# The first token tile arrives turned by a DMA transpose, the second tile's load changes queue, two weight loads become one, and a strip's first blocks are pulled forward

## The chip, the cores and the metric

The kernel runs on one core of one Trainium2 chip. The metric is the device time of one execution in microseconds (us). The kernel before takes 215.7 us (median of 6 executions, 215.33 to 216.21). Times inside an execution are counted from the span's start. One execution differs from the next by some tenths of a microsecond, so a profile (one execution) is used to find where time goes, and six executions in turn with the kernel before are used to say how much.

## The reference, cut to what matters

```python
def reference(...):                      # x: 1 x 2048 x 640, bf16
    g = sigmoid((x * gate_w).sum(-1, keepdims=True))
    a = A(x, ...)                        # complex state space: Bu = x @ B_bar, scan over time, y = h @ C + x * Dskip
    b = gelu(x @ w1 + b1) @ w2 + b2      # w1: 640 x 1728, w2: 1728 x 640
    return g * a + (1 - g) * b
```

The opening of the kernel computes the first 768 columns of `x @ w1` for the first 512 tokens. TensorE contracts over the partition axis, so it needs x turned (features on partitions), while x lies in memory with tokens on partitions. D = 640 features are five *strips* of 128. The 512 tokens are four *token tiles* of 128. A *turn* is a matmul with the identity that turns one 128x128 piece of x; VectorE or ScalarE then copies it out of PSUM.

## The kernel before: the parts that matter

The loads of the opening. `nc.sync` is SyncE's DMA queue, `nc.scalar` ScalarE's. `w1a[kd]` holds strip kd of the first 768 columns of w1 (192 KB), `w1b` the next 512, `w1c` the last 448 and one gate column.

```python
    w1b = [const.tile([P, cut2 - cut1], BF16, name=f"w1b_{kd}") for kd in range(KD)]
    w1c = [const.tile([P, n1c], BF16, name=f"w1c_{kd}") for kd in range(KD)]
    # ... cut ...
    load_x0(nc.sync, 0, 1, 0, KA * P)         # token tile 0, first 256 features (64 KB)
    load_w1a(nc.scalar, 0)                    # first strip's weights
    load_x0(nc.sync, 1, 2, 0, KA * P)         # token tile 1
    load_w1a(nc.scalar, 1)                    # second strip's weights
    load_x0(nc.sync, 2, 3, 0, KA * P)
    load_x0(nc.scalar, 0, H, KA * P, D)
    # ... cut: tile 3, w1a[2], three rows of parameters, the rest of x, w1a[3:5], parameters for the biases ...
    for kd in range(KD):
        nc.sync.dma_start(out=w1b[kd][:], in_=B_w1[kd * P:(kd + 1) * P, cut1:cut2])
    for kd in range(KD):
        nc.sync.dma_start(out=w1c[kd][:, 0:F - cut2], in_=B_w1[kd * P:(kd + 1) * P, cut2:F])
```

The order of TensorE's work. `turn_first(a, ..)` turns the first two strips of token tile a; `part(kd, a)` is six matmuls of 128 columns: strip kd of token tile a, for six blocks of output features.

```python
    pA = bank()
    for n in (512, 512, 512, 512, 512, 128, 128, 128, 128):          # warm-up, on constants
        nc.tensor.matmul(pA[:, 0:n], lhsT=ones(P), rhs=ones(n), start=True, stop=True)
    # ... cut ...
    turn_first(0, pA)
    # ... cut ...
    for _ in range(3):                                               # three more on constants
        nc.tensor.matmul(banks[0][:, 0:P], lhsT=ones(P), rhs=ones(P), ...)
    part(0, 0)
    turn_first(1, pA)
    part(1, 0)                                                       # the first user of w1a[1]
    turn_first(2, pA)
    part(0, 1)
    part(1, 1)
    turn_first(3, pA)
    part(0, 2)
    part(1, 2)
    nc.tensor.matmul(pA[:, 0:3 * KS], lhsT=prmA[:], rhs=ident[:, 0:3 * KS], ...)     # "prmA turn"
    # ... cut: the other turns and parts; these go on to part(2, 2) ...
    part(2, 3)
    # ... cut ...
    for kf in range(FA):                                             # FA = 6
        if kf == 3:
            nc.tensor.matmul(pA[:, 0:NB], lhsT=prmB[:], ...)         # "prmB turn"
            nc.vector.tensor_copy(out=colB[:], in_=pA[:, 0:NB])
            for j in range(KD):                                      # gate-column copies, out of PSUM bank pA
                nc.vector.tensor_copy(out=w1c[j][:, n1c - 1:n1c], in_=pA[:, j:j + 1])
        for kd in (4, 3):
            ff1_mm(banks[kf], 0, kf, kd, 0, CH, False, 3)
    # ... cut ...
    two_banks = [bank(), bank()]                                     # the second one is pA's bank again
    for kd in range(KD):
        for i in range(2):
            ff1_mm(two_banks[i], 0, FA + i, kd)                      # the first users of w1b
```

Of the kernel before, what the change touches and what calls it, by code (L numbers as in the profile page):

```python
# [12 lines left out]
BF16 = mybir.dt.bfloat16  # L13
# [3 lines left out]
P = 128  # L17
T = 2048
D = 640
F = 1728  # L20
CH = 512
NCH = T // CH
KD = D // P
# [6 lines left out]
HT = H * P  # L30
# [11 lines left out]
def kernel(  # L42
# [19 lines left out]
    nc = tc.nc  # L62
    x2d = A_x.flatten_outer_dims()
# [3 lines left out]
    const = ctx.enter_context(tc.tile_pool(name="const", bufs=1))  # L67
# [7 lines left out]
    def bank(dtype=F32):  # L75
        return ps.tile([P, CH * 4 // (4 if dtype == F32 else 2)], dtype, name="bank")
# [4 lines left out]
    cut2 = FB * P  # L81
    n1c = F - cut2 + 1
    xT = [const.tile([P, KD, CH], BF16, name=f"xT{c}") for c in range(NCH)]
# [1 line left out]
    w1a34 = const.tile([P, 2, cut1], BF16, name="w1a34")  # L85
    w1a += [w1a34[:, j, :] for j in range(2)]
    w1b = [const.tile([P, cut2 - cut1], BF16, name=f"w1b_{kd}") for kd in range(KD)]
    w1c = [const.tile([P, n1c], BF16, name=f"w1c_{kd}") for kd in range(KD)]
    w2_sb = const.tile([P, KF - 1, D], BF16, name="w2_sb")
    BT_re, BT_im = ([const.tile([P, KD, n * P], BF16, name=f"BT_{ri}{n}") for n in (KSA, KS - KSA)] for ri in ("re", "im"))  # L90
    CT_re = const.tile([P, KS, D], BF16, name="CT_re")
# [34 lines left out]
    def load_w1a(queue, kd):  # L126
        queue.dma_start(out=w1a[kd][:], in_=B_w1[kd * P:(kd + 1) * P, 0:cut1])
# [4 lines left out]
    KA = 2  # L132
    xn[0] = xnp.tile([P, TPC, D], BF16, name="xn")

    def load_x0(queue, a0, a1, d0, d1):
        queue.dma_start(out=xn[0][:, a0:a1, d0:d1], in_=x2d[a0 * P:a1 * P, d0:d1].rearrange("(a p) d -> p a d", p=P))

    load_x0(nc.sync, 0, 1, 0, KA * P)
    load_w1a(nc.scalar, 0)
    load_x0(nc.sync, 1, 2, 0, KA * P)  # L140
    load_w1a(nc.scalar, 1)
    load_x0(nc.sync, 2, 3, 0, KA * P)
    load_x0(nc.scalar, 0, H, KA * P, D)
# [12 lines left out]
    rows(nc.sync, prmB[0:KS, :], gate_w)  # L156
    for kd in range(KD):
        nc.sync.dma_start(out=w1b[kd][:], in_=B_w1[kd * P:(kd + 1) * P, cut1:cut2])
    for kd in range(KD):
        nc.sync.dma_start(out=w1c[kd][:, 0:F - cut2], in_=B_w1[kd * P:(kd + 1) * P, cut2:F])  # L160
    make_identity(nc, ident[:])
    HC = CH // 8
# [16 lines left out]
        nc.sync.dma_start(out=w2_sb[:, k0:k1, :], in_=B_w2[k0 * P:k1 * P, :].rearrange("(kf p) d -> p kf d", p=P))  # L179
    for h in range(2):  # L180
        nc.sync.dma_start(out=w2l[h * F_LAST:(h + 1) * F_LAST, :], in_=B_w2[(KF - 1) * P:F, :])
    nc.sync.dma_start(out=b2bc[:], in_=B_b2.rearrange("(o d) -> o d", o=1).to_broadcast([P, D]))
    nc.sync.dma_start(out=Dbc[:], in_=A_Dskip.rearrange("(o d) -> o d", o=1).to_broadcast([P, D]))
    nc.sync.dma_start_transpose(out=xT[2][:], in_=x2d[2 * CH:3 * CH, :])
# [32 lines left out]
    def pe(cols):  # L217
        ck.pe += cols / 2400.0 + 0.002
# [9 lines left out]
    pA = bank()  # L228
# [3 lines left out]
    def turn(p, col, a, kd):  # L232
        nc.tensor.matmul(p[:, col:col + P], lhsT=xn[0][:, a, kd * P:(kd + 1) * P], rhs=ident[:], start=True, stop=True,  # L233
                         skip_group_check=True)

    def turned(engine, p, col, a, k0, k1):
        dst = xT[0][:, k0:k1, a * P:(a + 1) * P]
        src = p[:, col:col + (k1 - k0) * P].rearrange("p (k t) -> p k t", t=P)
        if engine is nc.vector:
            nc.vector.tensor_copy(out=dst, in_=src)  # L240
        else:
            nc.scalar.activation(out=dst, in_=src, func=ACT.Identity)  # L242

    def turn_first(a, other):
        t = bank()
        turn(t, 0, a, 0)
        turned(nc.vector, t, 0, a, 0, 1)
        turn(other, a * P, a, 1)
        turned(nc.scalar, other, a * P, a, 1, 2)

    turn_first(0, pA)

    def col(name, dtype=F32, n=KS):
        return const.tile([P, n], dtype, name=name)
# [9 lines left out]
    def ff1_mm(p, c, kf, kd, t0=0, t1=CH, first=None, last=KD - 1):  # L264
        w, f0 = (w1a, 0) if kf < FA else (w1b, FA) if kf < FB else (w1c, FB)
        w = w[kd][:, (kf - f0) * P:(kf - f0 + 1) * P]
        nc.tensor.matmul(p[:, t0:t1], lhsT=w, rhs=xT[c][:, kd, t0:t1],  # L267
                         start=(kd == 0) if first is None else first, stop=(kd == last), skip_group_check=first is not None)
        pe(t1 - t0)
# [53 lines left out]
    banks = [bank() for _ in range(FA)]  # L323

    def strip(kd, t0, t1, first, f0=0, f1=FA):
        for kf in range(f0, f1):
            ff1_mm(banks[kf], 0, kf, kd, t0, t1, first, 3)
# [26 lines left out]
    def part(kd, a):  # L354
        strip(kd, a * P, (a + 1) * P, kd == 0)
# [28 lines left out]
    nc.vector.tensor_tensor(out=red, in0=u, in1=kk[:], op=ALU.subtract)  # L384
    part(2, 1)
    part(2, 2)
    part(2, 3)
    nc.scalar.activation(out=FSC[:, 0:KS, 0:NP], in_=red, func=ACT.Sin, scale=TWO_PI_M)
    nc.vector.scalar_tensor_tensor(out=ab, in0=red, scalar=-1.0, in1=red, op0=ALU.mult, op1=ALU.max)
    nc.scalar.activation(out=FSC[:, KS:2 * KS, 0:NP], in_=ab, func=ACT.Sin, scale=-TWO_PI_M, bias=halfpi[:])  # L390
    for kf in range(FA):
        if kf == 3:
            nc.tensor.matmul(pA[:, 0:NB], lhsT=prmB[:], rhs=ident[:, 0:NB], start=True, stop=True, skip_group_check=True)  # L393
            nc.vector.tensor_copy(out=colB[:], in_=pA[:, 0:NB])
            for j in range(KD):
                nc.vector.tensor_copy(out=w1c[j][:, n1c - 1:n1c], in_=pA[:, j:j + 1])
        for kd in (4, 3):
            ff1_mm(banks[kf], 0, kf, kd, 0, CH, False, 3)
    for kf in range(FA):
        ff1_act(banks[kf], 0, kf)  # L400
    two_banks = [bank(), bank()]
# [336 lines left out]
```

## Time and profile before

| | before |
|---|---|
| median of 6 executions | 215.7 us (215.33 to 216.21) |
| profiled execution, its span | 215.48 us, 213.7 us |
| TensorE busy | 210.0 us, 98% of the span |
| VectorE busy | 189.0 us, 88% |
| second strip's weights: issued, landed | 1.15 us, 4.28 us |
| first real block; first block of the second strip | 4.01 us; 4.69 us |

The busy table of the kernel before (engine, busy us, share of the span, instructions):

```profile
span 213.7 us, 3596 instructions
PE 210.0 (98%) x1407; PEld 126.1 (59%) x1407; DVE 189.0 (88%) x387; ACT 103.2 (48%) x186; POOL 1.0 (0%) x13
```

The chain of waits of the kernel before (start us, us, what) shows the opening's one hole, before the last blocks of the third strip:

```profile
8.68 0.39 ACT xT L242
...
9.10 0.30 DVE xT L240
...
9.45 1.79 PE bank L267 x12
```

ScalarE's copy, then VectorE's copy of token tile 3 must end first. And VectorE's timeline at the gate-column copies:

```profile
11.40 0.41 DVE L396 CAST w1c<-bank 128x1 bf16<-128x1 f32 x5
```

All five copies run at once; none waits for a load.

### The profile page before, as it was taken

What the parts mean: (1) busy time and instruction counts of PE and PEld (TensorE: products, weight loads), DVE (VectorE), ACT (ScalarE), POOL (GpSimd) and SP (SyncE); (2) the same over time, 40 slices, a digit from 0 to 9 for tenths busy, and PEclk for the clock granted to TensorE, in tenths of its full rate; (3) what the DMA queues carried; (4) which work ended last, traced back from release to release, by engine and by line L of the source; (5) the groups of instructions that cost most, each with busy time, mean ns of one, the idle gap of its engine ahead of it and who ended that gap; (6) DMA issues with size and microseconds to landing.
All of it is one profiled execution on the core that took longest, in us unless ns stands there. A gap on an engine that the chain in (4) does not pass through costs nothing.

```text
span 213.7 us, 3596 instructions
## 1 busy us (share of the span) xinstructions
PE 210.0 (98%) x1407; PEld 126.1 (59%) x1407; DVE 189.0 (88%) x387; ACT 103.2 (48%) x186; POOL 1.0 (0%) x13
## 2 busy tenths in 40 slices
PE   8999999999999999999999999999999999999994
PEld 5845444454576644775457777444457687676773
DVE  2689999999998999999999999999999999993153
ACT  3699856675758588203563210455682422305100
POOL 1000000000000000000000000000000000000000
DMA  6859999998000000051000005100000000100011
GB/s 196 236 133 182 228 172 267 337 204 219 1 0 0 3 0 0 17 178 67 0 0 3 0 0 187 61 0 2 3 0 14 0 3 31 61 34 0 0 66 61
DMA packets 31571, 15.84 MB, mean 74 GB/s; under 512 B 22978, under 2 KB 31554, under 8 KB 31554
## 3 DMA queue, kind: packets, MB, share of 16 engines
q1 hardware_dynamic: 30850, 14.99, 28.8%
q10 hardware_dynamic: 704, 0.62, 0.9%
q8 instruction: 11, 0.18, 0.4%
q14 instruction: 6, 0.05, 0.1%
HBM read 7.48 MB, written 2.62 MB: 47 GB/s over the span
## 4 chain that ended last, share of the span: by engine, by line
PE 98%; DVE 0%; ACT 0%; issue 0%
PE bank L605 27%; PE bank L267 26%; PE bank L664 20%; PE bank L546 20%; PE bank L230 1%; PE bank L621 1%; PE bank L293 1%; PE bank L233 1%; ACT xT L242 0%; DVE ot L669 0%; PE bank L358 0%; DVE xT L240 0%; PE bank L283 0%; PE bank L393 0%; PE bank L368 0%
## 5 line engine op out<-in xcount | busy, mean ns | idle before, releaser
L605 PE MATMUL bank<-w_sb,gel 128*128 128x384 bf16 (+1 forms) x416 | 57.9, 299 | 0.0
L605 PEld LDWEIGHTS <-gel 128*128 128x128 bf16 x416 | 40.3, 98 | 17.0 <-issue 0.8
L549 ACT ACTIVATE bu<-bank 128x512 bf16<-128x512 f32 x40 | 23.6, 597 | 37.6 <-PE bank L546 37.6
L272 ACT ACTIVATE gel<-bank,colB 128x512 bf16<-128x512 f32 x52 | 33.9, 692 | 11.1 <-PE bank L267 10.8
L664 PEld LDWEIGHTS <-hs 128*128 128x128 bf16 x330 | 31.7, 98 | 11.6
L500 DVE TENSOR_TENSOR_SCAN g<-r_c,carry,v 128x512 bf16<-128x512 f32 x30 | 37.2, 1269 | 0.0
L613 ACT ACTIVATE gb<-bank,gcol 128x384 f32<-128x384 f32 (+1 forms) x32 | 15.1, 525 | 33.6 <-PE bank L605 16.8
L267 PE MATMUL bank<-xT,w1a 128*128 128x512 bf16 (+1 forms) x174 | 28.1, 315 | 0.1
L664 PE MATMUL bank<-CT_im,hs 128*128 128x320 bf16 (+2 forms) x165 | 27.1, 295 | 0.0
L664 PE MATMUL bank<-CT_re,hs 128*128 128x320 bf16 (+2 forms) x165 | 27.1, 295 | 0.0
L669 DVE SCALAR_TENSOR_TENSOR ot<-bank,gcol,gb 128x320 bf16<-128x320 f32 (+2 forms) x33 | 17.4, 533 | 9.9 <-PE bank L664 9.5
L546 PE MATMUL bank<-xT,BT_re 128*128 128x512 bf16 x100 | 24.8, 379 | 0.0
L546 PE MATMUL bank<-xT,BT_im 128*128 128x512 bf16 x100 | 24.8, 379 | 0.0
L267 PEld LDWEIGHTS <-w1a 128*128 128x128 bf16 x174 | 14.5, 99 | 11.8 <-issue 0.2
L267 PE MATMUL bank<-xT,w1b 128*128 128x512 bf16 x80 | 17.9, 379 | 0.0
L546 PEld LDWEIGHTS <-BT_im 128*128 128x128 bf16 x100 | 9.8, 98 | 11.8
L579 DVE TENSOR_TENSOR bank<-xn,Dbc 128x320 f32<-128x320 bf16 (+2 forms) x33 | 14.5, 481 | 2.3 <-ACT gb L613 2.3
L546 PEld LDWEIGHTS <-BT_re 128*128 128x128 bf16 x100 | 9.6, 98 | 11.0
L481 DVE TENSOR_TENSOR v<-wa,wb 128x512 bf16<-128x512 bf16 x40 | 15.2, 421 | 0.6
L594 ACT ACTIVATE bank<-b2bc 128x384 f32<-128x384 bf16 (+1 forms) x24 | 11.7, 524 | 7.3 <-DVE ot L669 7.3
L481 DVE TENSOR_TENSOR wa<-TCOS,g 128x1024 bf16<-128x1024 bf16 x20 | 13.7, 685 | 0.1
L267 PE MATMUL bank<-xT,w1c 128*128 128x512 bf16 x60 | 13.7, 379 | 0.0
(99 smaller groups left out, 166.1 us busy)
## 6 DMA issues: line engine op xcount, KB each, us to landing
out_dram<-ot SPq DMA_DIRECT2D x15, 160.0 KB, 1.8
w_sb<-in_B_w_dram SPq DMA_DIRECT2D x1, 2080.0 KB
xn<-in_A_x_dram SPq DMA_DIRECT2D x3, 640.0 KB
w1b<-in_B_w_dram SPq DMA_DIRECT2D x5, 128.0 KB, 4.2
w1c<-in_B_w_dram SPq DMA_DIRECT2D x5, 112.0 KB, 4.9
w1a<-in_B_w_dram ACTq DMA_DIRECT2D x2, 192.0 KB, 3.1
w1a<-in_B_w_dram SPq DMA_DIRECT2D x1, 384.0 KB, 3.4
xn<-in_A_x_dram SPq DMA_DIRECT2D x4, 64.0 KB, 3.2
```

The source lines that it names most:

```text
L267: nc.tensor.matmul(p[:, t0:t1], lhsT=w, rhs=xT[c][:, kd, t0:t1], start=(kd == 0) if first is None else first, stop=(kd == last), skip_grou ...
L272: nc.scalar.activation(out=gel[c][:, kf, :], in_=p[:, :], func=ACT.Gelu_apprx_tanh, bias=b1_c[:, kf:kf + 1])
L481: nc.vector.tensor_tensor(out=o, in0=a, in1=b, op=op)
L500: nc.vector.tensor_tensor_scan(s["g"][:, ri, :], r_c[:, ks:ks + 1].to_broadcast([P, CH]), s["v"][:, ri, :], init, ALU.mult, ALU.add)
L546: nc.tensor.matmul(p[:], lhsT=BT[ks >= KSA][:, kd, (ks % KSA if ks < KSA else ks - KSA) * P:][:, 0:P], rhs=xT[c][:, kd, :], start=(kd == 0 ...
L549: nc.scalar.activation(out=bu[:, ri, :], in_=p[:], func=ACT.Identity)
L579: dve_now(ck.pe, 0.45, lambda: nc.vector.tensor_tensor(out=p[:, 0:d1 - d0], in0=xn[c][:, a, d0:d1], in1=Dbc[:, d0:d1], op=ALU.mult))
L594: nc.scalar.activation(out=v, in_=src, func=ACT.Identity)
L605: nc.tensor.matmul(p[:, col:col + d1 - d0], lhsT=gel[c][:, kf, a * P:(a + 1) * P], rhs=w2_sb[:, kf, d0:d1], start=False, stop=False, skip_ ...
L613: nc.scalar.activation(out=gbs[ti][:, d0:d1], in_=p[:, col:col + d1 - d0], func=ACT.Identity, scale=gcol[:, 1, ti:ti + 1])
L664: nc.tensor.matmul(p[:, 0:d1 - d0], lhsT=hs[c][:, j, lo:lo + P], rhs=CT[:, j % KS, d0:d1], start=False, stop=(j == 2 * KS - 1), skip_group ...
L669: nc.vector.scalar_tensor_tensor(out=ot[:, d0:d1], in0=p[:, 0:d1 - d0], scalar=gcol[:, 0, ti:ti + 1], in1=gbs[ti][:, d0:d1], op0=ALU.mult, ...
```

## The change

The intent: the first two turns and their copies leave the opening (the DMA brings token tile 0 already turned), the second token tile comes by ScalarE's queue, between the two weight loads, and three half blocks of the fifth strip fill the hole at 9.2 us. The plain copy of tile 0's 256 features, which the output stages need, is loaded later; two w1c loads become one, so the number of loads stays the same.

```diff
-    w1c = [const.tile([P, n1c], BF16, name=f"w1c_{kd}") for kd in range(KD)]
+    w1c = [const.tile([P, n1c], BF16, name=f"w1c_{kd}") for kd in range(3)]
+    w1c34 = const.tile([P, 2, n1c], BF16, name="w1c34")
+    w1c += [w1c34[:, j, :] for j in range(2)]
@@ the opening's loads
-    load_x0(nc.sync, 0, 1, 0, KA * P)
+    nc.sync.dma_start_transpose(out=xT[0][:, 0:KA, 0:P], in_=x2d[0:P, 0:KA * P])
     load_w1a(nc.scalar, 0)
-    load_x0(nc.sync, 1, 2, 0, KA * P)
+    load_x0(nc.scalar, 1, 2, 0, KA * P)
     load_w1a(nc.scalar, 1)
@@ after the w1b loads
-    for kd in range(KD):
+    nc.sync.dma_start(out=w1c34[:, :, 0:F - cut2], in_=B_w1[3 * P:KD * P, cut2:F].rearrange("(k p) f -> p k f", p=P))
+    for kd in range(3):
         nc.sync.dma_start(out=w1c[kd][:, 0:F - cut2], in_=B_w1[kd * P:(kd + 1) * P, cut2:F])
@@ later loads
+    load_x0(nc.sync, 0, 1, 0, KA * P)
@@ TensorE
-    turn_first(0, pA)
@@ before the last part of the third strip
+    AHEAD = 3
+    strip(KD - 1, 0, HT, False, 0, AHEAD)
     part(2, 3)
@@
-            ff1_mm(banks[kf], 0, kf, kd, 0, CH, False, 3)
+            ff1_mm(banks[kf], 0, kf, kd, HT if kd == 4 and kf < AHEAD else 0, CH, False, 3)
```

## The prediction

> **What bounds it now.** TensorE: busy 210.0 of 213.7 us (busy table); the chain of waits is 98% PE. Beyond the opening its only hole over 0.2 us is at 9.17-9.45 us (timeline): the last third-strip blocks wait for VectorE's copy of token tile 3, itself behind a ScalarE copy. Opening: warm-ups end at 3.3 us, when tile 0's rows land; two PE turns and two copies follow, and the first real block starts at 4.01 us. VectorE is nearly as full: from 11.3 to 191 us it idles once, 0.96 us (timeline, waits).
>
> **What the change does.**
> - Opening: two turns and two copies of tile 0 go; a 128x256 DMA transpose comes. The trace has that size (gelL): 1.17 us on SyncE's queue, 3.1 us to landing; free of traffic its last increment came 2.3 us after issue. Issued at 0.73 beside the first weight load (landed 3.5), I estimate a landing at 3.5-3.9. First block 4.01 -> about 3.8: gain 0.1-0.25 us. TensorE's own saving is two 128-column turns, 0.11 us. (The Trainium skill, "VectorE: DVE Perf Modes", the three transpose paths, gives 1309 ns by DMA against 390 ns on TensorE; here queue and landing make it longer, so it pays only because loading was waited for anyway.)
> - The hole: three 256-column blocks of strip five (3 x 109 ns, half of a 512-column block's 216 ns spacing) fill about 0.28 us, if their weights, which landed at 8.4, are there. SyncE's queue moves back 0.2-0.6 us (longer issue; each issue reuses the semaphore of the eighth before it, and the order changed), so they land at about 8.9, just in time. prmA's third row may cost 0-0.3 us the same way.
> - Opening gain on TensorE, net: about 0.3 us (0 to 0.5).
>
> **The hidden cost.** The fourth and fifth blocks of w1c become one tile, loaded by one DMA. VectorE writes the gate column into that tile; in the built program this copy now waits for that DMA's full count, where before it waited for none (11.4 us). In before the first w1c loads landed at 13.9 and 14.2: 15 of 16 increments came by 11.9-12.2, the last about 2 us later, because an instruction fetch of 16 KB held one DMA engine from 10.4 to 12.3 (packet list). The Trainium skill, "DMA: Bandwidth & Descriptors", on why a DMA increments by 16, says only the full 16 means all has landed; this trace agrees. So VectorE should stop at about 11.4 for 1 to 3 us, likely 2.3. Having no idle time to give back, it stays late until 191 us.
>
> **What lateness costs.** TensorE needs VectorE's seeds at the start of each output stage. Slack (timeline): seed done 84.2, needed 86.4; 121.0/123.0; 172.8/174.1. Smallest: 1.3 us. So time changes by about max(-gain, lateness - 1.3): with 2.3 us of lateness +1.0; with 1 us or less -0.3. The tables' copies on ScalarE move about 1 us; banks absorb that.
>
> **Prediction.** 216.5 us (before 215.99), range 215.3 to 217.6; faster by over 2%: 0.01; within 2%: 0.96; slower by over 2%: 0.03.
>
> **What would show it.** First block at 3.7-3.9; no hole before 9.5; VectorE idle at the gate-column copy, released by the w1c DMA, 1-3 us; output stages (around 86, 123, 174) preceded by TensorE waits for seeds, summing to 0-1.5 us, most at the third.
>
> **What would make it wrong.** The w1c DMA landing by 12.3, because the fetch falls elsewhere: then 215.6. The transpose landing after 4.1, the prmA row or fifth-strip weights late: opening gain gone. A late fourth-or-fifth w1b load (landed 13.6, needed 14.1) stalling TensorE. Hidden slack in VectorE that I read as full.

## More of the kernel before

TensorE is the bound, so a microsecond in which it stands, or works slower than it could, is a microsecond of the result. Its timeline in the opening (start us, us, engine and line, output from inputs, shape, count):

```profile
4.01 0.73 PE L267 MATMUL bank<-xT,w1a 128*128 128x128 bf16 x6
4.58 0.28 PE L233 MATMUL bank<-ident,xn 128*128 128x128 bf16 x2
4.69 0.50 PE L267 MATMUL bank<-xT,w1a 128*128 128x128 bf16 x6
...
5.29 0.83 PE L267 MATMUL bank<-xT,w1a 128*128 128x128 bf16 x12
5.96 0.28 PE L233 MATMUL bank<-ident,xn 128*128 128x128 bf16 x2
...
6.74 0.17 PE L368 MATMUL bank<-ident,prmA 128*128 128x15 bf16 x1
```

Matmuls overlap, so read rates from starts, not from the busy column. The twelve blocks of 5.29 take until 5.96: 0.67 us, or 56 ns each. The first six take 0.57 us, 95 ns each on average; read one by one in the trace, they start 107 ns apart until 4.58 us. So TensorE runs at half rate to 4.58 us and at full rate after it. The Trainium skill, "TensorE: Matmul & The Clock Gate", Part 1, section "What's actually happening", describes this: TensorE starts at half clock, and a free-running window of about 3.4 us of activity decides when it gets the full one. The spacings here (107 ns, then 56 ns, for 128 columns) agree.

## The result, and the profile after

The changed kernel takes 217.84 us (217.21 to 218.08, 6 executions) against 215.7 us; ratio 1.0095, 95% interval 1.0073 to 1.0117. A ratio in this document is the mean time of one kernel's runs over the mean of the other's in the same rounds, so it is not quite the ratio of the medians quoted. The change costs 2.1 us, and the time lies outside the predicted range of 215.3 to 217.6.

The busy table after:

```profile
span 215.8 us, 3582 instructions
PE 211.0 (98%) x1397; PEld 128.1 (59%) x1408; DVE 188.7 (87%) x386; ACT 102.7 (48%) x185; POOL 1.0 (0%) x13
PEclk9999999999999999999999999999999999999999
```

TensorE is busy 1 us longer. The row of the granted clock says full speed in every slice: it does not show the half rate that we are about to see. The trace's clock records begin only where the full clock begins (9.16 us here), and time without a record is counted as full. TensorE's timeline after:

```profile
3.92 0.80 PE L269 MATMUL bank<-xT,w1a 128*128 128x128 bf16 x6
4.51 0.42 PE L237 MATMUL bank<-ident,xn 128*128 128x128 bf16 x2
5.47 0.82 PE L269 MATMUL bank<-xT,w1a 128*128 128x128 bf16 x6 [0.54 <-DMA w1a<-in_B_w_dram]
...
6.30 1.49 PE L269 MATMUL bank<-xT,w1a 128*128 128x128 bf16 x12
7.58 0.42 PE L237 MATMUL bank<-ident,xn 128*128 128x128 bf16 x2
7.79 1.49 PE L269 MATMUL bank<-xT,w1a 128*128 128x128 bf16 x12
9.07 0.22 PE L370 MATMUL bank<-ident,prmA 128*128 128x15 bf16 x1
9.15 0.33 PE L237 MATMUL bank<-ident,xn 128*128 128x128 bf16 x3
9.31 0.50 PE L269 MATMUL bank<-xT,w1a 128*128 128x128 bf16 x6
```

Two things are new. TensorE stands before the second strip: its last matmul before starts at 4.62, the next at 5.47, and the profile names the second strip's weights. And the twelve blocks of 6.30 take until 7.58: 1.28 us, 107 ns each, where before they took 56 ns. Half rate now lasts until 9.15 us. The chain of waits after says how the weights came late (the chain reads about 0.15 us later than the timeline for TensorE, because it goes by ends):

```profile
0.73 0.38 ACTq L129
...
1.14 0.46 ACTq L138
...
1.62 3.81 DMA w1a<-in_B_w_dram
...
5.47 0.82 PE bank L269 x6
...
11.03 1.44 PE bank L269 x22
```

On ScalarE's queue the second strip's weights now come third, behind the first strip's weights (L129) and token tile 1 (L138). They are issued at 1.62 instead of 1.15 and land at 5.43 instead of 4.28. The last line shown answers to the hole of before: 22 blocks in one piece, no copy in the chain. The filling works.

SyncE's queue before, and then after:

```profile
0.73 1.84 SPq L136 DMA_DIRECT2D xn<-in_A_x_dram  x4
6.38 2.26 SPq L158 DMA_DIRECT2D w1b<-in_B_w_dram  x5
```

```profile
0.73 1.29 SPq L140 DMA_TRANSPOSE xT<-in_A_x_dram  x1
7.76 2.26 SPq L160 DMA_DIRECT2D w1b<-in_B_w_dram  x5
```

The transpose holds the queue for 1.29 us (a plain load for about 0.4), and by the w1b loads this queue is 1.4 us late. The transpose is not the only reason: in two kernels below that have token tile 1 on ScalarE's queue and no transpose, these loads start at 7.01 (e2) and 7.50 (e11). VectorE's timeline after, at the gate-column copies:

```profile
13.50 0.28 DVE L400 CAST w1c<-bank 128x1 bf16<-128x1 f32 x3
14.11 0.23 DVE L400 CAST w1c<-bank 128x1 bf16<-128x1 f32 x2 [0.33 <-DMA w1c<-in_B_w_dram]
```

This is the wait that the prediction announced, for the merged tile's load, but it is 0.33 us and not 1 to 3, because VectorE itself comes 2 us later.

Cut at TensorE's landmarks (starts in the two profiles), the 2.1 us lie here:

| stretch | before | after | difference |
|---|---|---|---|
| to the first block of the second strip | 4.69 | 5.47 | +0.78 |
| from there to the prmA turn | 2.05 | 3.60 | +1.55 |
| prmA turn to prmB turn | 4.33 | 4.10 | -0.23 |
| prmB turn to the first `BT` matmul (the stage after the opening) | 9.60 | 9.60 | 0 |
| from there to the last matmul | 190.06 | 190.06 | 0 |
| sum | 210.73 | 212.83 | +2.10 |

Everything after 13 us is only shifted. A standstill costs 0.78, the half rate 1.55, and the filled hole gives 0.23 back. (From start to start the standstill is 0.85 us; taking off the 0.11 us that the matmul before it needs at half rate leaves 0.74 idle.)

### The profile page after: what moved, and what is told of

It reads as the page before. It is cut to its first block, busy times and chain, and to the rows that moved or that the text cites. A ratio compares the mean times of both kernels' runs of the same rounds, so it can differ in the third digit from the quotient of the medians.

```text
span 215.8 us, 3582 instructions
## 1 busy us (share of the span) xinstructions
PE 211.0 (98%) x1397; PEld 128.1 (59%) x1408; DVE 188.7 (87%) x386; ACT 102.7 (48%) x185; POOL 1.0 (0%) x13
## 4 chain that ended last, share of the span: by engine, by line
PE 96%; DMA 2%; ACTq 0%; issue 0%; DVE 0%
PE bank L269 27%; PE bank L609 26%; PE bank L668 20%; PE bank L550 20%; DMA w1a<-in_B_w_dram 2%; PE bank L625 1%; PE bank L295 1%; PE bank L237 1%; ACTq L138 0%; ACTq L129 0%; DVE ot L673 0%; PE bank L285 0%; PE bank L370 0%; PE bank L397 0%
## 5 line engine op out<-in xcount | busy, mean ns | idle before, releaser
L269 PE MATMUL bank<-xT,w1a 128*128 128x512 bf16 (+2 forms) x173 | 29.6, 328 | 0.9 <-DMA w1a<-in_B_w_dram 0.5
L269 PEld LDWEIGHTS <-w1a 128*128 128x128 bf16 x177 | 16.2, 108 | 12.4 <-DMA w1a<-in_B_w_dram 0.8
```

Of the source, the lines that this page charges most:

```text
L269: nc.tensor.matmul(p[:, t0:t1], lhsT=w, rhs=xT[c][:, kd, t0:t1], start=(kd == 0) if first is None else first, stop=(kd == last), skip_grou ...
```

## The experiments

Three theories for the standstill and what follows it. *Order*: the weights are late because token tile 1 stands ahead of them in ScalarE's queue. *Transpose*: they are late because the transpose's traffic slows everything. *Clock*: the standstill itself is small, and costs more because it makes the full rate come later. After the first four runs a fourth was needed: *merged tile*, a second penalty that the first one hides.

One table has the landmarks of all profiled executions. "Weights" is when the last part of the second strip's weights landed; "full rate" is the first start from which 128-column matmuls come 56 ns apart (where that falls into a standstill, the first start after it); the three columns after are landmarks of TensorE as above. BT to the last matmul was 190.05 or 190.06 us in every kernel, but 190.22 in e8.

| kernel | weights | full rate | prmA turn | prmA to prmB | prmB to BT | profiled us |
|---|---|---|---|---|---|---|
| before | 4.28 | 4.58 | 6.74 | 4.33 | 9.60 | 215.48 |
| after | 5.43 | 9.15 | 9.07 | 4.10 | 9.60 | 217.61 |
| e1_weights_first | 4.22 | 4.61 | 7.34 | 4.32 | 10.72 | 217.21 |
| e2_no_transpose | 5.95 | 6.0 | 7.90 | 4.06 | 10.25 | 217.08 |
| e3_transpose_alone | 4.14 | 9.53 | 9.46 | 4.37 | 9.60 | 218.32 |
| e4_filler | 5.77 | 4.0 | 7.72 | 4.19 | 10.77 | 217.53 |
| e5_strip_alone | 4.21 | 5.63 | 7.08 | 4.06 | 9.60 | 215.52 |
| e6_w1c_merged | 4.34 | 6.31 | 7.43 | 4.33 | 9.81 | 216.47 |
| e8_merged_gate_from_sbuf | 4.55 | 5.35 | 7.03 | 4.34 | 9.59 | 215.99 |
| e9_after_unmerged | 5.75 | 10.05 | 9.39 | 4.31 | 9.60 | 218.20 |
| e7_weights_first_unmerged | 4.09 | 4.33 | 7.31 | 4.06 | 9.60 | 215.88 |
| e10_filler_unmerged | 5.86 | 3.98 | 7.82 | 4.07 | 9.60 | 216.38 |
| e11_order_alone | 6.40 | 6.45 | 8.36 | 4.33 | 9.60 | 217.08 |
| e12_strip_three_fillers | 4.25 | 5.23 | 7.10 | 4.05 | 9.60 | 215.56 |
| e13_standstill_alone | 4.12 | 3.60 | 8.03 | 4.33 | 9.60 | 216.75 |
| e14_standstill_filled | 4.11 | 3.98 | 7.80 | 4.33 | 9.59 | 216.50 |
| e15_early_pair_filled | 4.17 | 6.10 | 7.85 | 4.05 | 9.60 | 216.39 |

All fifteen kernels are correct, all were timed in five rounds, and "before" was 215.65, 215.79, 215.71 and 215.57 us in the four sets of runs (e1 to e4; e5, e6, e8, e9; e7, e10, e11, e12; e13 to e15). The sets ran on three different chips, so times of different sets are compared only where the difference is far larger than these 0.2 us.

### e1_weights_first: the changed kernel with the old order on ScalarE's queue

```diff
-    load_x0(nc.scalar, 1, 2, 0, KA * P)
     load_w1a(nc.scalar, 1)
+    load_x0(nc.scalar, 1, 2, 0, KA * P)
```

> The changed kernel, but ScalarE's queue issues both weight loads before the second token tile, as in before; the DMA transpose stays. In the changed kernel the second weight load (w1a, second strip) landed at 5.43 us instead of 4.31, TensorE stood still for it and then ran at half speed until 9.1 us. Theory QUEUE ORDER (the 64 KB put ahead of it and its later issue delay it): lands by 4.4 us, second strip starts by 4.8 us, time 215.2 to 216.0. Theory TRANSPOSE (the transpose on SyncE's queue holds up what ScalarE's queue issues after it): still lands after 4.9 us, time 217 or more. Theory of my prediction (VectorE late through the merged w1c tile): if TensorE starts on time, VectorE waits 1 to 3 us at the gate-column copies and the time is 216 to 217.

Measured: 217.89 us (217.2 to 218.28), ratio 1.0102 (1.0086 to 1.0119). The weights land at 4.22, the full rate is there within the first six blocks (from 4.61), and the prmA turn is 1.7 us earlier than in the changed kernel. And the time is the same. The gain was given back at 13 us, which is where TensorE waits in this kernel (engine, line, what it waited for: us in total, times, longest):

```profile
PE bank L269 <- DVE w1c L400: 0.9, 1, 0.9
PE bank L269 <- DMA xT<-in_A_x_dram: 0.7, 1, 0.7
```

The second line is the transpose, landing at 4.43 here. The first is new: a w1b block waits for a gate-column copy of VectorE. So the order is what made the weights late, and something else keeps the time where it was.

### e2_no_transpose: the changed kernel with token tile 0 loaded and turned as before

```diff
-    nc.sync.dma_start_transpose(out=xT[0][:, 0:KA, 0:P], in_=x2d[0:P, 0:KA * P])
+    load_x0(nc.sync, 0, 1, 0, KA * P)
...
+    turn_first(0, pA)
```

> The changed kernel without the transpose: tile 0's rows come by SyncE's queue and are turned on TensorE as in before; the second tile stays on ScalarE's queue ahead of the second weight load. QUEUE ORDER: the second weight load lands after 5.0 us, time 217 or more. TRANSPOSE: it lands by 4.7 us (64 KB more ahead of it, about 0.25 us at the 300 GB/s of that stage), time 215.3 to 216.2. Merged-tile theory: with TensorE on time, VectorE waits 1 to 3 us at the gate-column copies, time up to 217.

Measured: 217.37 us (216.66 to 218.28), ratio 1.0083 (1.0062 to 1.0104). The weights still land at 5.95 and TensorE still stands before the second strip (0.9 us put down to the weights). The theory that the transpose's traffic makes the weights late falls. In this execution the full rate came during the standstill, and again TensorE waited for a gate-column copy, 0.5 us.

### e3_transpose_alone: the kernel before with the transpose and nothing else

```diff
-    load_x0(nc.sync, 0, 1, 0, KA * P)
+    nc.sync.dma_start_transpose(out=xT[0][:, 0:KA, 0:P], in_=x2d[0:P, 0:KA * P])
...
+    load_x0(nc.sync, 0, 1, 0, KA * P)      # after the w2 loads
...
-    turn_first(0, pA)
```

> Before, with the transpose alone: tile 0's first 256 features turned by DMA, its rows loaded later, all else as in before (second tile on SyncE's queue behind the transpose). TRANSPOSE: the second weight load lands after 4.9 us, or the second tile's rows do, and the time is 217 or more. QUEUE ORDER: weights land by 4.5 us; the second tile's rows, issued at about 2.0 us instead of 1.2, land at about 5.0 instead of 4.06, so TensorE still waits up to 0.5 us; time 215.8 to 216.8.

Measured: 216.31 us, ratio 1.0059 (1.0026 to 1.0091), in two groups: four executions at 216.22 to 216.33, two at 218.02 and 218.32. The profile is one of the late ones. The weights land at 4.14, the transpose at 4.33, and TensorE waits for it (0.6 us) and then for token tile 1 behind it in SyncE's queue (0.5 us). In that execution the full rate came at 9.53 us. So the transpose alone does not pay: it lands about 1 us after a plain load of the same piece (3.29 in the kernel before).

### e4_filler: the changed kernel with eight blocks on constants where TensorE stands

```diff
     turn_first(1, pA)
+    for _ in range(8):
+        nc.tensor.matmul(banks[0][:, 3 * P:4 * P], lhsT=ones(P), rhs=ones(P), start=True, stop=True, skip_group_check=True)
     part(1, 0)
```

> The changed kernel with eight idle 128-column matmuls (ones by ones, into columns that are overwritten later) between the second tile's turns and the second strip, so that TensorE does not stand still while the second weight load is awaited. CLOCK theory (the standstill of 0.85 us keeps TensorE at half speed 4.5 us longer, about 1.5 us of the loss; the wait itself is 0.8): spacing of 128-column matmuls falls from 107 to 56 ns by 6 us, time about 216.3. If the half speed has nothing to do with the standstill: spacing stays 107 ns until 9 us, time 217.8 as the changed kernel.

Measured: 217.59 us (217.39 to 217.7, 4 executions), ratio 1.0089 (1.0076 to 1.0103). TensorE's timeline:

```profile
4.00 0.49 PE L269 MATMUL bank<-xT,w1a 128*128 128x128 bf16 x6 [0.20 <-DMA xT<-in_A_x_dram]
...
4.45 0.63 PE L364 MATMUL bank<-const-bfloat16-1.0 128*128 128x128 bf16 x8
5.82 0.51 PE L269 MATMUL bank<-xT,w1a 128*128 128x128 bf16 x6 [0.74 <-DMA w1a<-in_B_w_dram]
...
13.23 0.38 PE L269 MATMUL bank<-xT,w1b 128*128 128x512 bf16 x1
14.61 1.25 PE L269 MATMUL bank<-xT,w1b 128*128 128x512 bf16 x5 [1.00 <-DVE w1c L402]
```

In this execution TensorE has its full rate already at 4.00, before the fillers begin, so the profile cannot show that the fillers brought it. What it does show is the worth of an early full rate: the prmA turn is 1.35 us earlier than in the changed kernel (7.72 against 9.07) although the weights land 0.34 us later. And it shows where that goes. Between the first and the second w1b block 1.38 us pass (blocks of this size come about 216 ns apart elsewhere). VectorE's timeline has the reason:

```profile
12.24 0.28 DVE L402 CAST w1c<-bank 128x1 bf16<-128x1 f32 x3
14.33 0.23 DVE L402 CAST w1c<-bank 128x1 bf16<-128x1 f32 x2 [1.81 <-DMA w1c<-in_B_w_dram]
```

The fourth copy writes into the merged tile and waits for its load, which lands at 14.30. The copies read PSUM bank pA, and the second w1b bank is that same bank. TensorE may not start there before the fifth copy has read it. This is the second penalty: it holds the stage after at 22.2 to 22.7 us, whether or not the opening is late. In the changed kernel, where TensorE gets there 1.3 us later, it is hidden.

### e5_strip_alone: the kernel before with the fifth strip's early blocks

```diff
     part(2, 2)
+    AHEAD = 3
+    strip(KD - 1, 0, HT, False, 0, AHEAD)
     part(2, 3)
...
-            ff1_mm(banks[kf], 0, kf, kd, 0, CH, False, 3)
+            ff1_mm(banks[kf], 0, kf, kd, HT if kd == 4 and kf < AHEAD else 0, CH, False, 3)
```

> Before with one part alone: three half blocks of the fifth strip put before the last third-strip blocks, to fill the standstill at 9.17 to 9.45 us. The weights of the fifth strip landed at 8.4 us in before, so they are there. Prediction's term: 0.25 us faster, about 215.4 where before is 215.65; the gap before the last third-strip blocks shrinks from 0.35 us spacing to under 0.25 of anything but work. Rival (the hole is a latency that moves along behind the inserted work): no change.

Measured: 215.58 us (215.46 to 215.76), ratio 0.9994 (0.9982 to 1.0006). The stretch from prmA to prmB shrinks by 0.27 us, as predicted for this part. In the time nothing can be told from zero; in the profiled execution the full rate came 1 us later than in the kernel before's, and the prmA turn 0.34 us later with it, which is more than the hole gives back.

### e6_w1c_merged: the kernel before with the two w1c loads merged

The edit is the first and third hunk of the change.

> Before with one part alone: the fourth and fifth w1c blocks in one tile loaded by one DMA, issued before the other three. BANK theory (formed from the experiments with the weights first and with the filler, where TensorE stood 0.9 to 1.5 us before its second w1b matmul, released by the gate-column copy): that copy waits for the DMA, and the bank that it reads is the one TensorE needs next; so TensorE, which would need it at about 12.5 us, waits until the DMA has landed, at 13.9 to 14.3 us: 1.2 to 1.7 us slower, about 217.1. Theory of my prediction (no direct wait; only VectorE's lateness at the output stages, less 1.3 us of slack): 216.0 to 216.9, TensorE without a gap at 12 to 14 us and with gaps at about 86, 123 and 174 us.

Measured: 216.52 us (216.29 to 217.16), ratio 1.0042 (1.0026 to 1.0059). VectorE waits 0.8 us for the merged load (landed 13.20), and the weight load of a w1b block waits 0.5 us for the copy; prmB to BT grows by 0.22 us. Of the 0.99 us between the two profiled executions that is a quarter. The rest, 0.69 us, is lost before the prmA turn, with full rate at 6.31. It would probably not have been won with an earlier full rate: the wait ends with the landing at 13.20, so a TensorE that came 0.69 us earlier would have waited that much longer at the same bank (an estimate from this profile, not a run).

### e8_merged_gate_from_sbuf: the same, with the copies reading SBUF

```diff
-                nc.vector.tensor_copy(out=w1c[j][:, n1c - 1:n1c], in_=pA[:, j:j + 1])
+                nc.vector.tensor_copy(out=w1c[j][:, n1c - 1:n1c], in_=colB[:, j:j + 1])
```

> The merged w1c tile on before, but the gate columns are copied from the SBUF copy of the column values and no longer from the PSUM bank, so TensorE gets that bank as soon as the column copy is done, while VectorE still waits for the merged load. BANK theory alone: no gap on TensorE at 12 to 14 us, time near before (215.5 to 215.9) as far as the later slack holds. My prediction's slack reading: VectorE stops 1.5 to 2.5 us and stays late, the first output stages wait for seeds, time = before + (lateness - 1.3 us), so 215.9 to 216.9, with TensorE gaps at about 86, 123 or 174 us.

Measured: 216.44 us (215.99 to 216.55), ratio 1.0031 (1.0017 to 1.0045). VectorE still waits 0.9 us for the load, but TensorE does not wait for VectorE any more, and prmB to BT is back at 9.59. This shows the path of the cost: the PSUM bank. It also tests the prediction's path, VectorE's lateness reaching the output stages: no wait for VectorE's seeds appears there with 0.9 us of lateness. That is under the slack of 1.3 us that the prediction read, so it neither breaks nor makes the rule. (The 0.16 us more between BT and the last matmul go to one pause before 84 us that the profile puts down to instruction issue.) In time the kernel gains next to nothing over e6_w1c_merged, so what its executions lose stays unexplained. The profiled one is the fastest of the six; the five others took 216.09 to 216.55 and left no trace, so a later loss through VectorE is not ruled out there.

### e9_after_unmerged: the changed kernel with five separate w1c loads

> The changed kernel with the five w1c blocks again in tiles and loads of their own. If the merged tile costs time in the changed kernel: faster by 0.5 us or more. If the late second weight load and the half clock set the time there and merely hide the merged tile's wait (0.33 us of VectorE in its trace): the same 217.2 to 218.1 in executions where the clock comes at 9 us; executions where the clock comes earlier, if there are any, would be 216 to 217.

Measured: 218.02 us (217.53 to 218.41, 5 executions), ratio 1.0105 (1.0088 to 1.0121). Taking away the merged tile alone gives nothing. Its profile has the standstill, and no wait at 13 us:

```profile
5.79 0.82 PE L266 MATMUL bank<-xT,w1a 128*128 128x128 bf16 x6 [0.82 <-DMA w1a<-in_B_w_dram]
...
6.62 1.49 PE L266 MATMUL bank<-xT,w1a 128*128 128x128 bf16 x12
```

The twelve blocks of 6.62 are busy 1.49 us, as in the changed kernel, where they take 0.83 us at full rate. So each of three repairs alone (order, filler, separate tiles) leaves the time within 0.3 us of the changed kernel. Either none of them is a cause, or there are two penalties of about the same size side by side in time, of which only the longer counts. Runs that repair two things at once decide.

### e7_weights_first_unmerged: old order and separate tiles together

> Two-penalty theory (queue order of the second weight load, and the merged last weight tile, each cost about 2 us and hide behind one another): with both undone, the second weight load lands by 4.4 us, TensorE does not stand before its second w1b block at about 13 us, the table stage starts at 21.2 to 21.6 us instead of 22.4, and the time is 216.2 to 216.8 us in most runs (what is left is the transpose, which lands late). Single-cause theory (only the order, or only the transpose, matters, and the merged tile is innocent): the time stays where the same kernel with the merged tile was, 217.9.

Measured: 216.05 us, ratio 1.0044 (1.0011 to 1.0077); four executions at 215.87 to 216.05, two at 217.61 and 218.01. The profile (215.88) has the weights at 4.09, full rate at 4.33, no wait for VectorE, prmB to BT 9.60. The two repairs that did nothing alone gain 1.8 us together. The two late executions look like those of e3_transpose_alone; no profile of one of them was taken.

### e10_filler_unmerged: filler and separate tiles together

> The changed kernel with fillers in the standstill and with five separate last weight tiles. Two-penalty theory: fillers alone (217.6) and separate tiles alone (218.0) each gained nothing, together they gain over 1 us: full clock from about 4 us, no stand at 13 us, table stage at 21.2 to 21.8 us, time 216.2 to 216.9. If the clock is not what the fillers act through, or the merged tile does not set the floor, the time stays at 217.4 to 218.

Measured: 216.2 us (216.04 to 216.38), ratio 1.0027 (1.0013 to 1.0041). From 217.59 and 218.02 to 216.2. TensorE and VectorE in this kernel, to set beside those of the filler alone:

```profile
13.21 2.54 PE L266 MATMUL bank<-xT,w1b 128*128 128x512 bf16 x11
```

```profile
12.22 0.41 DVE L399 CAST w1c<-bank 128x1 bf16<-128x1 f32 x5
```

The w1b blocks start at the same 13.2 us as with the filler alone and then go through without a break. From e9_after_unmerged it differs by the eight blocks alone (the two ran in different sets), and its six executions all lie more than 1.1 us below e9's five. In its profile, too, the full rate was there before the fillers began; what they do has to be read from the spread of the executions, and the last three runs are for that.

### e11_order_alone: the kernel before with token tile 1 moved to ScalarE's queue

```diff
-    load_x0(nc.sync, 1, 2, 0, KA * P)
+    load_x0(nc.scalar, 1, 2, 0, KA * P)
```

> The kernel before with one edit: the second token tile's load moves to ScalarE's queue, ahead of the second weight load. Order theory: that weight load lands at 5.2 us or later (4.3 before), TensorE stands 0.6 to 1.2 us before the second strip; where the clock then stays half until about 9 us the time is about 217.7, where it rises early about 216.4, so runs of one kernel spread between those two. Rival (the order needs the transpose's company to hurt): landing by 4.6 us and 215.7.

Measured: 217.64 us, ratio 1.0088 (1.006 to 1.0117): 216.64, 216.7, 217.08 and three of 218.2 to 218.28. One moved line of 64 KB, with nothing else changed, gives the whole loss:

```profile
6.45 0.51 PE L267 MATMUL bank<-xT,w1a 128*128 128x128 bf16 x6 [1.46 <-DMA w1a<-in_B_w_dram]
```

The weights land at 6.40, later than in the changed kernel. The rival (the order hurts only beside the transpose) falls.

### e12_strip_three_fillers: an attempt at a version that beats both

```diff
     # the kernel before with the fifth strip's early blocks, and:
-    for _ in range(3):
+    for _ in range(6):
         nc.tensor.matmul(banks[0][:, 0:P], lhsT=ones(P), rhs=ones(P), ...)
```

> A version that might beat both: the kernel before with the fifth strip's early blocks, and three more 128-column filler blocks before the first real block, to close the 0.27 us gap there. If the gap is what made the clock rise at 5.6 us in the run with the strip alone, it now rises by about 4.5 us and the time is 215.2 to 215.4; if the arrival is just chance or the gap does not matter, 215.5 to 215.7 as with the strip alone.

Measured: 215.53 us (215.38 to 216.18), ratio 1.0 (0.9982 to 1.0017). The gap before the first block is gone, and the full rate comes at 5.23 us, not at the 4.5 that the idea behind it asked for: a gap of 0.27 us was not what kept it away in e5_strip_alone. No version was found that beats the kernel before by more than the measurement can tell.

### e13_standstill_alone: the kernel before with a standstill and no load moved

```diff
     turn_first(1, pA)
+    nc.tensor.matmul(banks[0][:, 3 * P:4 * P], lhsT=ones(P), rhs=xn[0][:, 0, KA * P:(KA + 1) * P], ...)
     part(1, 0)
```

The added matmul waits for a piece of x that ScalarE's queue brings third, as before; its product is overwritten.

> The kernel before with a standstill of TensorE from about 4.7 to 5.6 us and no load moved. Clock theory (a standstill inside an activity window makes the window fail): full rate either by about 5.6 us or not before 8, nothing in between; times in two groups, near 216.5 (standstill alone) and near 218.0 (standstill and late rate), with at least two of six executions in the upper one. Rival (the late rate comes from the moved loads or their traffic): all executions near 216.5, full rate by 6.4 us as in the kernel before and its relatives.

Measured: 216.44 us, ratio 1.0045 (1.0009 to 1.0081): five executions at 216.01 to 216.75 and one at 218.36. No execution of the kernel before was above 216.38 in any set. So a standstill alone can bring the upper time, with every load where it was; but once in six, not the two that were expected. The profile is an early one: full rate at 3.60, before the standstill, which was 1.7 us long and not 0.9.

### e14_standstill_filled: the same with eight blocks on constants

The eight blocks of e4_filler, ahead of the matmul that waits.

> The same with eight blocks on constants in the standstill. Clock theory: no execution in the upper group, full rate by about 7 us at the latest, times from 216.3 to 217.0 in one group. Rival: the same two groups, or the same single one, as without the fillers.

Measured: 216.51 us (216.31 to 216.91), ratio 1.0039 (1.0019 to 1.0058). No execution in the upper group, as the clock theory has it; against one in six without the blocks, this pair alone decides nothing. In the profile the rate was full, so the eight blocks cover only 0.45 us of the wait; at half rate they would cover 0.86 us (8 times 107 ns). They fill the wait best in the executions that need it.

### e15_early_pair_filled: e7 with blocks on constants in both its waits

```diff
-    for _ in range(3):
+    for _ in range(10):
         nc.tensor.matmul(banks[0][:, 0:P], lhsT=ones(P), rhs=ones(P), ...)
     part(0, 0)
+    for _ in range(5):
+        nc.tensor.matmul(banks[0][:, 3 * P:4 * P], lhsT=ones(P), rhs=ones(P), ...)
     turn_first(1, pA)
```

> The changed kernel with the old order, separate tiles, and blocks on constants in both waits of its opening (ten before the first real block, five before the second token tile's turns). Clock theory: the late executions of the same kernel without fillers (217.6 and 218.0, two of six) do not appear, all six at 215.9 to 216.4. Rival (fillers do not matter): again some at 217.5 or above.

Measured: 216.18 us (215.73 to 216.65), ratio 1.0022 (1.0001 to 1.0044). The two late executions of e7 have no counterpart. The profile is of an execution whose full rate came at 6.1 us, late but with no second delay: TensorE had work throughout, and the prmA turn is at 7.85 (9.07 in the changed kernel). This is the changed kernel without its two faults, and it is still no faster than the kernel before.

Taken together, over executions at 217.5 us or more: kernels with an unfilled standstill and separate tiles had 13 of 29 (e3 2 of 6, e7 2 of 6, e9 5 of 5, e11 3 of 6, e13 1 of 6); kernels with blocks on constants in it and separate tiles had 0 of 18 (e10, e14, e15). If filling had no effect, so uneven a split would come by chance less than once in a thousand (Fisher's exact test on these counts; the line at 217.5 was drawn after seeing the times). Without e9, whose five are all late, it is 8 of 24 against 0 of 18, about one in 150.

## Why the prediction was wrong, point by point

**What it had right.** TensorE is the bound. The transpose landed at 3.88, inside the estimated 3.5 to 3.9, and the first real block moved from 4.01 to 3.92 (predicted about 3.8, so 0.09 us gained and not 0.2). The fifth strip's blocks filled the hole: -0.23 us here, -0.27 alone. VectorE does stop at the gate-column copies for the merged load, 0.33 us in the changed kernel and 1.8 us where TensorE is not late itself. The mechanism it names for this wait, that the copy needs the load's full count, is in the runs: the load lands at 14.08 and 14.30, and the copies follow at 14.11 and 14.33. (The Trainium skill, "DMA: Bandwidth & Descriptors", on why a DMA increments its semaphore by 16, was cited for it, and these runs agree.) That it forecast a small loss at all (216.5, against the 215.99 it had for the kernel before) is luck: that loss was to come in the output stages, and the stretch from BT to the last matmul takes 190.06 us in both kernels.

**The step that failed.** "Opening gain on TensorE, net: about 0.3 us (0 to 0.5)." The opening costs 2.1 us. The prediction costed what the change does to token tile 0 and passed over what moving token tile 1 does to the load behind it. The diff shows that `load_x0(nc.scalar, 1, ...)` is put between the two weight loads. The Trainium skill, "DMA: Bandwidth & Descriptors", section "Queues, rings and completion order", says that within a queue each DMA engine takes descriptors in order. Applied to the second weight load, needed at 4.69 and landing at 4.28 in the kernel before, this leaves 0.4 us of slack for 64 KB more in front. In the six kernels with token tile 1 ahead (after, e2, e4, e9, e10, e11) the weights land at 5.43 to 6.40; in the others at 4.09 to 4.55. This is shown, with and without the transpose. Why it is so much is not shown: 64 KB at the 196 GB/s of the profile's first slice would be about 0.33 us (an estimate), and 0.47 us of later issue adds to it; 1.2 to 2.1 us were measured. The traces show one thing more. Between 3.0 and 4.5 us all DMA traffic together ran at 148 GB/s in the changed kernel and at 314 in the kernel before; it was 109 to 208 in every kernel with token tile 1 on ScalarE's queue (these six, and e1, e7 and e15, where it comes after the weights) and 250 to 358 in the others. In the changed kernel's packet records most packets of this load take 65 ns, as before, but between 3.2 and 4.2 us some take several hundred (152 ns on the mean, against 69). What slows them was not settled.

**The second step that failed: the rate was taken as given.** The prediction costs TensorE's work at the spacings of the profile before and never asks how long the half rate lasts. It lasted to 9.15 us instead of 4.58. That is 1.55 us of the 2.1, so a standstill of 0.85 us cost nearly three times its length. Shown, by the counts of executions above: with work in the standstill the late times do not appear, and a standstill without any moved load (e13) can bring one.

Why a standstill of 0.85 us can do that is worked out here from the profiles; no run controls it. The skill's clock page describes windows of about 3.4 us that run freely, so that they do not start with the kernel. The packed traces hold clock records that no view of the profile prints, in every profiled execution but the kernel before's. Each of these 16 has one record of full clock in the kernel. It starts within 0.1 us of where the spacings change, or in the wait just before, and it lasts 208.213 or 211.626 us: 61 or 62 times 3.413 us. So the changes lie on a grid of 3.413 us, and the windows can be counted back from the start of the record. Adding up the time in a window in which TensorE had no matmul (all of the time before its first one included) gives this for six of the kernels:

| kernel | last window at half rate, us | idle in it, us | the window before it | idle in it, us |
|---|---|---|---|---|
| after | 5.75 to 9.16 | 0.06 | 2.34 to 5.75 | 1.07 |
| e9 | 6.62 to 10.03 | 0.06 | 3.21 to 6.62 | 1.38 |
| e3 | 6.11 to 9.52 | 0.05 | 2.69 to 6.11 | 1.45 |
| e1 | 1.14 to 4.55 | 0.87 | -2.27 to 1.14 | 3.04 |
| e2 | 1.94 to 5.35 | 0.76 | -1.47 to 1.94 | 2.24 |
| e13 | 0.17 to 3.59 | 0.59 | (before the kernel) | |

In all 16, the window after which the full clock came held 0.05 to 0.87 us of idle time, and each earlier one that overlaps TensorE's work 0.97 us or more. In the changed kernel the window from 2.34 to 5.75 held 1.07 us: 0.32 before the first real block and 0.74 in the standstill. Without the standstill it would have held 0.32, well inside what sufficed elsewhere; with it, another whole window had to pass. A standstill that falls into the window less unluckily costs only itself, as in e2 and e13. This is why one kernel has two groups of times (e3, e7, e11, e13). How often each group comes is not explained by it (e9 has five late ones of five). That the profiled execution of e4, e7, e10, e11 and e13 was an early one is luck.

**The third: the hidden cost went the wrong way.** The prediction sent VectorE's wait to the output stages with 1.3 us of slack. The gate-column copies read a PSUM bank that TensorE's second w1b bank reuses, with about 0.8 us of slack (in the kernel before the copies end at 11.81, and that block starts at 12.61). Where TensorE is on time, it stands there and loses 0.65 to 1.17 us between prmB and BT (e1, e2, e4). Reading the copies from SBUF takes that wait away (e8), and separate tiles take it away too (e7, e10). In the changed kernel it costs nothing on top, because TensorE is already late.

**How the terms add.** They do not: the opening's lateness and the merged tile's floor overlap, so the longer one counts. That is why the three single repairs (e1, e4, e9) changed the time by -0.25 to +0.2 us, and two pairs of them (e7, e10) gained 1.6 to 1.8 us. What is left of e7's early group against the kernel before, some 0.3 us, may go with the transpose, which lands at 4.29 there and at 4.3 to 4.4 in e1 and e3.

**What stays open.** Why the weights come 1.2 to 2.1 us late behind 64 KB. Why all DMA traffic slows from 3.0 to 4.5 us when token tile 1 goes by ScalarE's queue. Why e8 loses 0.65 us when its profile shows no wait. What sets the clock windows' position in an execution, and where between 0.87 and 0.97 us of idle time the limit lies.

## What to carry to other kernels

When a change moves a load between queues, look up every load behind it in its new queue and how much slack that one had; here the moved load was not late, the one after it was. A short standstill in the first microseconds can cost several times its length through the clock, if it is the one that makes a window of 3.41 us too idle (here, somewhere above 0.87 us of idle time in all): read TensorE's rate from the spacing of its starts before and after, and fill an unavoidable wait there with blocks on constants. When undoing a suspected cause changes nothing, look where the gain was given back before acquitting it, and undo two at once.

## What the Trainium skill lacked or had wrong

- "TensorE: Matmul & The Clock Gate", Part 1: its window of about 3.4 us is right (3.413 us here), but it puts the change of rate at 0.5 us more or less from run to run. Here the full rate came at 3.60 to 6.31 us in profiles with no standstill over 0.4 us before it, with TensorE's first matmul at 0.77 us each time (3.60 in e13, 6.31 in e6). It does not say how much idle time a window may hold and still bring the full clock: 0.87 us was not too much here, 0.97 us was. Its rule of "no PE-idle gaps >~3.4µs" does not protect a kernel whose full clock has not come yet: here a standstill of 0.85 us held it back to 9.15 us, and late executions vanished with the standstill filled (13 of 29 against 0 of 18). It calls the ramp under 1% of a span: 1.55 us of 215 is that, and it was most of what this change did.
- "DMA: Bandwidth & Descriptors", "Queues, rings and completion order" and "Issuing engines are not separate DMA queues": the order within a queue is there, its price is not, and the second section makes the choice of queue sound like issue time alone. One 64 KB load placed ahead on the same queue made the next 192 KB load land 1.15 us (after) to 2.1 us (e11) later, and with it on that queue all traffic from 3.0 to 4.5 us ran at 109 to 208 GB/s instead of 250 to 358.
- "VectorE: DVE Perf Modes", the three transpose paths: it gives 1309 ns for the DMA's way with 128x128, and neither the time on the issuing queue nor that to landing. Here a transpose of 128x256 held SyncE's queue 1.29 us (a plain load 0.4), pushed the w1b loads on that queue back by 1.3 us when it was the only change (6.38 to 7.70, e3), and landed 3.15 to 3.7 us after issue; the plain load of the same piece landed 2.56 us after issue.
- No page says that a profile's row of the granted clock counts time without a record as full speed. Here the row reads full in every slice, while blocks came 107 ns apart until 9.15 us and the first clock record starts at 9.16 us; the kernel before's trace has no clock record at all.
